# A scalar on 128 partitions: a broadcast load at the head of the load queue instead of a matmul

## The chip, the core and the metric

The kernel runs on one core of one Trainium2 chip. The metric is the device time of one execution in microseconds (us); the time of a kernel is the median of several executions.

## What is computed

`x` and `fx` have the shape (512, 32, 640) in bf16, `alpha` has one bf16 element. The result has the shape and type of `x`:

```python
def reference(x, fx, alpha):
    return x + alpha * fx
```

Each of the three large arrays is 10,485,760 elements, 20.97 MB. Two are read and one is written, 62.9 MB in all.

## The kernel before

Each array is seen as 128 rows of 81,920 elements, one row for each SBUF partition, and cut along the row into five chunks of `CHUNK = 16384` elements. A chunk is a tile of 128 x 16384 bf16, 32 KB in each partition and 4096 KB in all. The tiles of `x` come from a pool `xs` with four buffers, those of `fx` from a pool `fs` with two. The result overwrites the tile of `x`, and this tile is stored.

For chunk k, `compute(k)` is one VectorE instruction (L69, `scalar_tensor_tensor`), which reads `f_t`, multiplies by the scalar `a_f`, adds `x_t` and writes `x_t`. The scalar has to stand in each of the 128 partitions as an f32 value. The last chunk is computed and stored in two halves.

All ten loads (L59 for `x`, L63 for `fx`) and all six stores (L80) are issued by SyncE, in an order that is written out by hand, as no scheduler moves anything:

```python
    load_x(0)
    load_f(0)
    load_x(1)
    load_f(1)
    load_x(2)
    compute(0)
    load_f(2)
    store(0)
    load_x(3)
    compute(1)
```

It goes on in the same way to `store(4, 0, 2)` and `store(4, 1, 2)`. SyncE waits ahead of an issue where that issue needs it: a load of `fx` for the compute that frees its buffer, the fifth load of `x` for the first store, and a store for its compute.

Ahead of all this, `alpha_to_lanes` brings the scalar to the partitions. ScalarE issues a DMA that loads the one element into one partition (L20); VectorE fills a row of 128 ones (L22); TensorE multiplies the two, which leaves alpha in 128 partitions of PSUM (L24); VectorE copies it to `a_f` in SBUF (L26). The lines L120 and L131 are those of the program's start and end.

Of the kernel before, what the change touches and what calls it, by code (L numbers as in the profile page):

```python
# [1 line left out]

# [4 lines left out]

ACT = mybir.ActivationFunctionType
ALU = mybir.AluOpType
F32 = mybir.dt.float32  # L10
BF16 = mybir.dt.bfloat16

CHUNK = 16384


def alpha_to_lanes(nc, consts, psum, alpha, eng):

    P = nc.NUM_PARTITIONS
    a_1 = consts.tile([1, 1], alpha.dtype, name="a_1")
    eng.dma_start(out=a_1[:], in_=alpha[None, :])  # L20
    ones = consts.tile([1, P], alpha.dtype, name="ones")
    nc.vector.memset(ones[:], 1.0)  # L22
    a_ps = psum.tile([P, 1], F32, name="a_ps")
    nc.tensor.matmul(a_ps[:], ones[:], a_1[:], start=True, stop=True)  # L24
    a_f = consts.tile([P, 1], F32, name="a_f")
    nc.vector.tensor_copy(out=a_f[:], in_=a_ps[:])  # L26
    return a_f


@with_exitstack  # L30
def kernel(
    ctx: ExitStack,
    tc: tile.TileContext,
    x: bass.AP,
    fx: bass.AP,
    alpha: bass.AP,
    out: bass.AP,
):
    nc = tc.nc
    P = nc.NUM_PARTITIONS  # L40
    xv = x.flatten_outer_dims().rearrange("(p n) d -> p (n d)", p=P)
    fxv = fx.flatten_outer_dims().rearrange("(p n) d -> p (n d)", p=P)
    ov = out.flatten_outer_dims().rearrange("(p n) d -> p (n d)", p=P)
    F = xv.shape[1]
    K = F // CHUNK
    assert K * CHUNK == F and K == 5

    consts = ctx.enter_context(tc.tile_pool(name="consts", bufs=1))
    psum = ctx.enter_context(tc.tile_pool(name="psum", bufs=1, space=bass.MemoryType.PSUM))
    xs = ctx.enter_context(tc.tile_pool(name="xs", bufs=4))  # L50
    fs = ctx.enter_context(tc.tile_pool(name="fs", bufs=2))
    ctx.enter_context(tc.manual_schedule())

    a_f = alpha_to_lanes(nc, consts, psum, alpha, nc.scalar)
    xt, ft = {}, {}

    def load_x(k):
        xt[k] = xs.tile([P, CHUNK], x.dtype, tag="x", name="x_t")
        nc.sync.dma_start(out=xt[k][:], in_=xv[:, bass.ts(k, CHUNK)])  # L59

    def load_f(k):
        ft[k] = fs.tile([P, CHUNK], fx.dtype, tag="f", name="f_t")
        nc.sync.dma_start(out=ft[k][:], in_=fxv[:, bass.ts(k, CHUNK)])  # L63

    def compute(k, parts=1):
        n = CHUNK // parts
        for j in range(parts):
            s = bass.ts(j, n)
            nc.vector.scalar_tensor_tensor(  # L69
                out=xt[k][:, s],  # L70
                in0=ft[k][:, s],
                scalar=a_f[:],
                in1=xt[k][:, s],
                op0=ALU.mult,
                op1=ALU.add,
            )

    def store(k, j=0, parts=1):
        n = CHUNK // parts
        nc.sync.dma_start(  # L80
            out=ov[:, k * CHUNK + j * n : k * CHUNK + (j + 1) * n],
            in_=xt[k][:, bass.ts(j, n)],
# [12 lines that stand above are left out]
    load_f(3)  # L95
    store(1)
    load_x(4)
    compute(2)
    load_f(4)
    store(2)  # L100
    compute(3)
    store(3)
    compute(4, 2)
    store(4, 0, 2)
    store(4, 1, 2)


# [1 line left out]
_INS = ['x', 'fx', 'alpha']  # L109
_OUTS = [((512, 32, 640), 'bfloat16')]  # L110


# [23 lines left out]
```

## Time and profile before

| | |
|---|---|
| median of 4 runs | 152.68 us (152.46 to 153.14) |
| the profiled execution's own time | 152.58 us |
| its span, from the first to the last instruction | 150.8 us |
| busy: VectorE, TensorE | 86.9 us, 0.2 us |
| moved by DMA | 62.92 MB, mean 417 GB/s over the span |
| 128x16384 instruction of L69 | 17.28 us each, four of them |
| 128x8192 instruction of L69 | 8.75 us each, two of them |

The profile is one execution; its own time and its span differ by what lies before the first and after the last instruction. In the lines of the profile, SPq and ACTq are the instruction queues of SyncE and ScalarE, where DMAs are issued, and DVE is VectorE, PE and PEld are TensorE's matmuls and weight loads. The duration beside a DMA issue is that of the issue alone; the data moves afterwards, on 16 DMA engines. q1 is the DMA queue that SyncE feeds and q10 the one that ScalarE feeds.

### The profile page before, as it was taken

How to read it: one execution, taken by the hardware profiler on the slowest of the kernel's cores; microseconds unless marked ns; L12 is line 12 of the kernel's file. 1: busy time of each engine (PE TensorE's matmuls, PEld its weight loads, DVE VectorE, ACT ScalarE, POOL GpSimd, SP SyncE). 2: the span in 40 equal slices, each digit the busy share in tenths (PEclk: the TensorE clock that was granted, in tenths of full speed). 3: DMA queues.
4: the chain of work that ended last, by engine and by line, in shares of the span. 5: the costliest groups of instructions: out<-in, count | busy, mean ns of one | idle time of the engine just before them, and what ended most of it. 6: DMA issues, size and time to landing. Idle time of an engine off the chain costs nothing.

```text
span 150.8 us, 85 instructions
## 1 busy us (share of the span) xinstructions
PE 0.2 (0%) x1; PEld 0.1 (0%) x1; DVE 86.9 (58%) x8; POOL 0.2 (0%) x4
## 2 busy tenths in 40 slices
PE   0000000000000000000000000000000000000000
PEld 0000000000000000000000000000000000000000
DVE  0000009999679998399991006999900089997000
POOL 0000000000000000000000000000000000000000
DMA  6999999999999999899999999999999999998994
GB/s 217 435 426 443 426 417 417 452 443 435 435 452 417 426 417 391 365 435 443 435 435 417 417 417 435 452 452 426 435 426 435 417 426 426 452 443 387 435 435 196
DMA packets 2306, 62.92 MB, mean 417 GB/s; under 512 B 258, under 2 KB 258, under 8 KB 258
## 3 DMA queue, kind: packets, MB, share of 16 engines
q1 hardware_dynamic: 2304, 62.92, 97.9%
q10 hardware_dynamic: 2, 0.00, 0.0%
HBM read 41.94 MB, written 20.97 MB: 417 GB/s over the span
## 4 chain that ended last, share of the span: by engine, by line
DMA 56%; DVE 29%; DVEq 6%; issue 0%; SPq 0%
DMA f_t<-in_fx_dram 56%; DVE x_t L69 29%; DVEq L131 6%; SPq L59 0%; DVEq L69 0%
## 5 line engine op out<-in xcount | busy, mean ns | idle before, releaser
L69 DVE SCALAR_TENSOR_TENSOR x_t<-f_t,a_f,x_t 128x16384 bf16<-128x16384 bf16 (+1 forms) x6 | 86.6, 14440 | 49.7 <-DMA f_t<-in_fx_dram 49.7
L26 DVE COPY a_f<-a_ps 128x1 f32<-128x1 f32 x1 | 0.2, 159 | 1.1 <-PE a_ps L24 1.1
L22 DVE MEMSET ones<- 1x128 bf16 x1 | 0.2, 165 | 0.8 <-PEq L120 0.8
L24 PE MATMUL a_ps<-a,ones 1*128 1x1 bf16 x1 | 0.2, 159 | 1.9 <-DMA a<-in_alpha_dram 1.9
L120 POOL MEMSET const-bfloat16-1.0<- 128x1 bf16 x1 | 0.1, 101 | 0.0
L120 POOL MEMSET const-uint8-127<- 128x1 uint8 x1 | 0.1, 101 | 0.0
L24 PEld LDWEIGHTS <-ones 1*128 1x128 bf16 x1 | 0.1, 99 | 1.0 <-DVE ones L22 1.0
L120 POOL MEMSET const-float32-0.0<- 128x1 f32 x1 | 0.1, 98 | 0.2 <-issue 0.2
L120 POOL MEMSET const-float32-1.0<- 128x1 f32 x1 | 0.1, 98 | 0.0
## 6 DMA issues: line engine op xcount, KB each, us to landing
x_t<-in_x_dram SPq DMA_DIRECT2D x5, 4096.0 KB, 34.8
f_t<-in_fx_dram SPq DMA_DIRECT2D x5, 4096.0 KB, 32.2
out_dram<-x_t SPq DMA_DIRECT2D x4, 4096.0 KB, 36.6
out_dram<-x_t SPq DMA_DIRECT2D x2, 2048.0 KB, 15.2
a<-in_alpha_dram ACTq DMA_DIRECT2D x1, 0.0 KB
```

What stands on the lines that cost most here:

```text
L22: nc.vector.memset(ones[:], 1.0)
L24: nc.tensor.matmul(a_ps[:], ones[:], a_1[:], start=True, stop=True)
L26: nc.vector.tensor_copy(out=a_f[:], in_=a_ps[:])
L69: nc.vector.scalar_tensor_tensor(out=xt[k][:, s], in0=ft[k][:, s], scalar=a_f[:], in1=xt[k][:, s], op0=ALU.mult, op1=ALU.add,)
L120: nc = _bacc.Bacc("TRN2", target_bir_lowering=False, num_devices=1)
L131: with _tile.TileContext(nc) as tc:
```

## The change

`alpha_to_lanes` no longer uses TensorE. One DMA reads the single element of alpha 128 times and writes it to one bf16 column `a_b` of 128 partitions, and VectorE copies this column to `a_f` in f32. The DMA is issued by SyncE instead of ScalarE, and as `alpha_to_lanes` is called first, its issue comes ahead of `load_x(0)` on the same queue. The row of ones, the matmul and the PSUM pool are gone. The order of all loads, computes and stores is as it was. The lines after the function stand five lines higher: L54, L58, L64 and L75 for what was L59, L63, L69 and L80.

```diff
-def alpha_to_lanes(nc, consts, psum, alpha, eng):
+def alpha_to_lanes(nc, consts, alpha, eng):
 
     P = nc.NUM_PARTITIONS
-    a_1 = consts.tile([1, 1], alpha.dtype, name="a_1")
-    eng.dma_start(out=a_1[:], in_=alpha[None, :])
-    ones = consts.tile([1, P], alpha.dtype, name="ones")
-    nc.vector.memset(ones[:], 1.0)
-    a_ps = psum.tile([P, 1], F32, name="a_ps")
-    nc.tensor.matmul(a_ps[:], ones[:], a_1[:], start=True, stop=True)
+    a_b = consts.tile([P, 1], alpha.dtype, name="a_b")
+    eng.dma_start(out=a_b[:], in_=alpha.to_broadcast((P, 1)))
     a_f = consts.tile([P, 1], F32, name="a_f")
-    nc.vector.tensor_copy(out=a_f[:], in_=a_ps[:])
+    nc.vector.tensor_copy(out=a_f[:], in_=a_b[:])
     return a_f
...
     consts = ctx.enter_context(tc.tile_pool(name="consts", bufs=1))
-    psum = ctx.enter_context(tc.tile_pool(name="psum", bufs=1, space=bass.MemoryType.PSUM))
...
-    a_f = alpha_to_lanes(nc, consts, psum, alpha, nc.scalar)
+    a_f = alpha_to_lanes(nc, consts, alpha, nc.sync)
```

## The prediction, made before the changed kernel was run

> **What bounds the kernel now.** I read the page's header, the slices and the queues first, to see which resource is never idle.
>
> ```profile
> span 150.8 us, 85 instructions
> PE 0.2 (0%) x1; PEld 0.1 (0%) x1; DVE 86.9 (58%) x8; POOL 0.2 (0%) x4
> DMA  6999999999999999899999999999999999998994
> GB/s 217 435 426 443 426 417 417 452 443 435 435 452 417 426 417 391 365 435 443 435 435 417 417 417 435 452 452 426 435 426 435 417 426 426 452 443 387 435 435 196
> ...
> q1 hardware_dynamic: 2304, 62.92, 97.9%
> q10 hardware_dynamic: 2, 0.00, 0.0%
> ```
>
> A slice is 150.8/40 = 3.77 us. The 16 DMA engines are busy from the first slice to the last; VectorE is busy 58%. All data is on one queue, q1, that of SyncE: 62.92 MB. From slice 2 to slice 39 the rate is about 425 GB/s, so the bytes alone need 62.92/0.425 = 148 us of the 150.8. The two weak slices at the ends are the start-up and the completion, and a delay at the start can only matter if nothing later has slack that takes it up.
>
> The second view is the groups with what they wait for, and the chain of work that ended last.
>
> ```profile
> L69 DVE SCALAR_TENSOR_TENSOR x_t<-f_t,a_f,x_t 128x16384 bf16<-128x16384 bf16 (+1 forms) x6 | 86.6, 14440 | 49.7 <-DMA f_t<-in_fx_dram 49.7
> ...
> L26 DVE COPY a_f<-a_ps 128x1 f32<-128x1 f32 x1 | 0.2, 159 | 1.1 <-PE a_ps L24 1.1
> DMA f_t<-in_fx_dram 56%; DVE x_t L69 29%; DVEq L131 6%; SPq L59 0%; DVEq L69 0%
> ```
>
> VectorE waited 49.7 us for `f_t` and never for `a_f` after the start. The chain names VectorE for 29%, yet in that time the queue has work. I count what SyncE has issued against what has moved. Five loads (21.0 MB) are issued in the first 3.2 us and last until 21.0/0.425 = 49 us; the next issues come at 40.2 us, when the first compute ends. By 79.9 us, when the last `f_t` load goes out, 11 transfers (46.1 MB) are issued and about 33 MB have moved. At 129.8 us, when the first half of the last store is released, 14 transfers (58.7 MB) are issued and 128 x 0.427 = 55 MB have moved. So the queue does not run dry until the last half store, issued at 138.5 us, and **the stream of transfers is one serial resource from its first packet to its last**.
>
> The third view is the timeline of the start.
>
> ```profile
> 0.73 0.38 SPq L59 DMA_DIRECT2D x_t<-in_x_dram  x1
> 0.73 0.49 ACTq L20 DMA_DIRECT2D a<-in_alpha_dram  x1
> 0.81 0.17 DVE L22 MEMSET ones<- 1x128 bf16 x1 [0.81 <-PEq L120]
> 1.03 0.10 PEld L24 LDWEIGHTS <-ones 1*128 1x128 bf16 x1 [1.03 <-DVE ones L22]
> 1.16 0.42 SPq L63 DMA_DIRECT2D f_t<-in_fx_dram  x1
> 1.64 0.42 SPq L59 DMA_DIRECT2D x_t<-in_x_dram  x1
> 1.92 0.16 PE L24 MATMUL a_ps<-a,ones 1*128 1x1 bf16 x1 [1.92 <-DMA a<-in_alpha_dram]
> ...
> 2.12 0.16 DVE L26 COPY a_f<-a_ps 128x1 f32<-128x1 f32 x1 [1.14 <-PE a_ps L24]
> ...
> 22.92 17.28 DVE L69 SCALAR_TENSOR_TENSOR x_t<-f_t,a_f,x_t 128x16384 bf16<-128x16384 bf16 x1 [20.64 <-DMA f_t<-in_fx_dram]
> ```
>
> The columns are start, duration, engine, line and operation. SyncE issues the first load of `x` at 0.73 us, beside ScalarE's issue of alpha. `a_f` is ready at 2.28 us; its first reader starts at 22.92 us. When do the loads begin to move? Stretches of a tenth of a microsecond (last columns: clock, DMA share, GB/s) put the first data packets of 32 KB at 1.7 to 2.1 us, that is about 1.0 us after the issue starts:
>
> ```profile
> 1.60:1.70 0.10, 0.00 (x0) 0.00 (x0) 0.00 (x0) 0.00 (x0) 1.00 0.00 0
> 1.70:1.80 0.10, 0.00 (x0) 0.00 (x0) 0.00 (x0) 0.00 (x0) 1.00 6.85 1966
> ```
>
> (A packet is booked whole where it starts, hence a share above 1.)
>
> **What the Trainium skill says.** All from its page "DMA: Bandwidth & Descriptors".
> - Section "Issuing engines are not separate DMA queues": DMAs of several issuing engines run on the same 16 DMA engines, and a second issuer "will only save the time on the sequencer it takes to initiate the DMA". The trace agrees: ScalarE's 0.49 us lie beside SyncE's first 0.38 us. This saving is what the change gives up.
> - Section "Why a DMA increments its semaphore by 16 and not by 1": a copy of 128 partitions is split over 16 engines, a [1, 1] scalar runs on one. The counts agree: q10 has 2 packets (data and semaphore), and q1 has 2304 = 16 transfers x (128 rows + 16 semaphore packets).
> - Section "Measured", under "Bandwidth": 4 KB to 128 partitions takes 0.68 us on the DMA engines (for DMAs issued by GpSimd). No small 128-partition transfer is in the trace of before; I use this as a price.
>
> **The change part by part.**
> 1. Removed: the memset of `ones` (0.17 us), the weight load (0.10), the matmul (0.16), the wait for it (1.1), the PSUM tile. All of it is over by 2.3 us and hidden under the first two loads, for which VectorE waits until 22.92. Worth 0. If that cover were gone it would be some 1.4 us on VectorE.
> 2. The copy to `a_f` (0.16 us) now waits for the broadcast. That lands at about 0.73 + 1.19 (issue to landing of the scalar, 1.92 - 0.73) + 0.68 = 2.6 us, with 20 us to spare. VectorE holds nothing else before it. Cost 0.
> 3. One DMA issue moves from ScalarE's queue to the head of SyncE's and so ahead of all 16 issues there; `x` 0 to `x` 2 all start later by it. POOL's four memsets are not passed. The pitch of issues on SyncE at the start is 1.16 - 0.73 = 0.43 and 1.64 - 1.16 = 0.48 us, ScalarE's issue took 0.49. I take **0.45 us**. Bounds: the shortest and longest issue on SyncE in the trace, 0.33 and 0.73 us.
> 4. The scalar's single packet becomes 128 packets of 2 bytes and 16 for the semaphore, nine on each of the 16 engines, ahead of the first data packet. They can start where the first load's packets do now, at 1.7 us, and the price of 0.68 us takes them to 2.38. The first load's packets are ready at 1.70 + 0.45 = 2.15. What sticks out is 2.38 - 2.15 = **0.23 us**. Bounds: 0, if nine packets pass within the 0.45 us (50 ns each), and about 1.1 us if the engines start the load only after the broadcast has landed (case C below). A gain is not in this term: packets are only added to q1.
> 5. Buffers and waits: the order of SyncE's issues and the waits for computes and for freed buffers stay the same. The removed PSUM tile frees nothing that is waited for.
>
> Sum: 0 + 0 + 0.45 + 0.23 = **+0.68 us**. As the queue always holds a backlog, nothing later absorbs it: the landings of `f_t`, the computes and the stores shift together. The profiled execution took 152.58 us (1.78 us around its span); it would take 153.26. It lies 0.10 under the median of the four runs, 152.68, so for the median I say **153.36 us**. That is +0.45%; a measurement of this kernel can tell about 0.3%, or 0.46 us, from no change, so the effect is not far beyond what can be seen.
>
> **The rivals.**
> - B, hidden at the start. After the first packets at 1.7 to 2.5 us no further one starts until 3.25 us, though a 32 KB packet needs only 32768 B/(425/16 GB/s) = 1.23 us. The first ended at 1.7 + 1.23 = 2.93 at the earliest, most next ones start in 3.50 to 3.75, so the start-up has some 0.4 us of slack of its own. If that pause is a first-access cost that the tiny packets pay instead, 0.68 - 0.4 leaves +0.28: 152.96 us, no visible change. Against it: the pause may well follow the first large packets wherever they start.
> - C, a stall of the rings. If the 2-byte writes are slow, or each engine's semaphore write, which has to follow its data, holds up what lies behind it, the load's packets start only when the broadcast has landed, about 2.6 us, and their own latency after that is only partly hidden. Landing instead of 1.7 costs 0.9, and up to 0.6 us of the 1.0 between issue and first packet again: +1.5, 154.18 us. Against it: in the steady stream semaphore packets follow each transfer and the rate stays near 425.
> - D, faster. The rate dips where the 16 engines fall out of step: slices 16 and 17 (391 and 365 GB/s) and slice 37 (387) lose (39 + 65 + 43)/430 x 3.77 = 1.3 us. Slice 37, 135.7 to 139.5 us, lies where the last store is released with little backlog left. If alpha's packet on a second queue, on one engine only, is what sets this engine back at the start, an even load on all 16 would shrink the dips. It decides once it gains more than the 0.46 us of the bound and what step 3 and 4 still cost, 0.28 with the start as in B, together 0.74 us. With two thirds of the 1.3 gone the balance is 0.28 - 0.9 = about -0.62: 152.06 us. For it: only that a single slow engine delays every landing. Against it: one packet of 2 bytes is small beside 120 packets of 32 KB per engine, and nothing ties the dips to it.
> - That the change does not do what it says: the broadcast may be issued on SyncE at no more than the scalar's cost and run on few engines. The order of issues in the changed program has it first, so this ends in A or B.
>
> **How the numbers follow.** A (+0.68) 0.50, B (+0.28) 0.25, C (+1.5) 0.13, D (-0.62) 0.12. Hence slower by over 0.3%: A and C, 0.63; within 0.3%: B, 0.25; faster: D, 0.12. A alone spans 152.68 + 0.33 = 153.01 to 152.68 + 0.73 + 0.23 = 153.64. The range takes in B down to the undisturbed scatter of the runs (lowest 152.46) and C with its bound, and leaves D out: 152.5 to 154.3.
>
> **What would show it.** Right: the first line of the timeline is the issue of `a_b` on SyncE at 0.73, the first load's issue is at about 1.18, the first large packets at about 2.4, the first compute at about 23.6, and every later compute about 0.7 later with no new wait; the small packets on q1 grow by 144 (258 - 2 + 144 = 400) and q10 is gone. Wrong at step 3: an issue of the broadcast over 0.73 us or under 0.33. Wrong at step 4: large packets that start at 2.15 or before, or after 3 us. Wrong about the serial stream: a first compute that is later and a last store that is not. Wrong altogether: a last compute earlier than 121.07 us.

## The result and the profile after

Over 42 executions of the changed kernel and 61 of the kernel before, the medians are 153.10 and 152.69 us: +0.41 us. The ratio is 1.0029, 95% interval 1.0019 to 1.0039, that is 0.29 to 0.60 us slower in this round (a second round, below, shows less). The profiled executions took 152.85 and 152.58 us, both a little below their medians.

The page of the changed kernel, its totals, slices, queues, chain and groups:

```profile
span 151.1 us, 81 instructions
DVE 86.7 (57%) x7; POOL 0.2 (0%) x4
DMA  5999999999999999999999999999999999999995
GB/s 139 382 425 443 416 416 417 425 460 443 451 425 434 417 416 416 417 416 416 434 469 451 451 416 417 416 417 416 451 460 443 451 416 416 417 416 430 425 443 230
...
q1 hardware_dynamic: 2448, 62.92, 97.5%
...
DMA f_t<-in_fx_dram 56%; DVE x_t L64 29%; DVEq L126 6%; SPq L54 0%; SPq L20 0%; DVEq L64 0%
L64 DVE SCALAR_TENSOR_TENSOR x_t<-f_t,a_f,x_t 128x16384 bf16<-128x16384 bf16 (+1 forms) x6 | 86.5, 14439 | 48.2 <-DMA f_t<-in_fx_dram 48.2
```

The bound is the same: the DMA engines are busy in every slice and VectorE waits for `f_t`. TensorE is gone from the list, q10 from the queues, and q1 has 2448 - 2304 = 144 more packets, as counted. Three slices tell of the change. The first moves 139 GB/s instead of 217: the stream starts later. Slices 16 and 17, which were 391 and 365, are 416 and 417: **the dip is gone at this scale**, and the sum of the prediction had nothing for that. Slice 37 rises too, from 387 to 430, but from the start of the fifth compute to the end of the span both kernels take 29.7 us, so it is worth nothing here.

The timeline of the start and of the large computes:

```profile
0.72 0.54 SPq L20 DMA_DIRECT2D a_b<-in_alpha_dram  x1
1.32 0.56 SPq L54 DMA_DIRECT2D x_t<-in_x_dram  x1
...
3.94 0.15 DVE L22 CAST a_f<-a_b 128x1 f32<-128x1 bf16 x1 [3.94 <-DMA a_b<-in_alpha_dram]
24.06 17.28 DVE L64 SCALAR_TENSOR_TENSOR x_t<-f_t,a_f,x_t 128x16384 bf16<-128x16384 bf16 x1 [19.97 <-DMA f_t<-in_fx_dram]
...
43.46 17.29 DVE L64 SCALAR_TENSOR_TENSOR x_t<-f_t,a_f,x_t 128x16384 bf16<-128x16384 bf16 x1 [2.11 <-DMA f_t<-in_fx_dram]
...
63.08 17.29 DVE L64 SCALAR_TENSOR_TENSOR x_t<-f_t,a_f,x_t 128x16384 bf16<-128x16384 bf16 x1 [2.34 <-DMA f_t<-in_fx_dram]
```

The kernel before has the second and third compute here:

```profile
42.31 17.28 DVE L69 SCALAR_TENSOR_TENSOR x_t<-f_t,a_f,x_t 128x16384 bf16<-128x16384 bf16 x1 [2.10 <-DMA f_t<-in_fx_dram]
62.60 17.29 DVE L69 SCALAR_TENSOR_TENSOR x_t<-f_t,a_f,x_t 128x16384 bf16<-128x16384 bf16 x1 [3.01 <-DMA f_t<-in_fx_dram]
```

And the stretches of a tenth of a microsecond in which the data of the changed kernel starts (before: 1.70):

```profile
2.40:2.50 0.10, 0.00 (x0) 0.00 (x0) 1.00 0.07 0
2.50:2.60 0.10, 0.00 (x0) 0.00 (x0) 1.00 5.81 1311
```

The first load is issued 0.59 us later (1.32 against 0.73), its packets start 0.8 us later, and the first compute starts 1.14 us later (24.06 against 22.92). The records of single packets in the two traces show where the rest comes from: the 2-byte packets run from 2.0 to 3.5 us, and the first sixteen packets of 32 KB start at 2.5 to 3.7 us, where it was 1.7 to 2.4. The first of them is 0.8 us late, the sixteenth 1.3. The second compute is still 1.15 late. The third, at 63.08, is only 0.48 late, and the last two 0.32 and 0.36 (92.19 against 91.87, 121.43 against 121.07). So the start cost more than forecast, and 0.67 us of it came back between the second and the third compute. The kernel before shows why in the same stretch (clock, DMA share and GB/s are the last three columns):

```profile
57.00:58.00 1.00, 0.00 (x0) 0.00 (x0) 1.00 (x1) 0.00 (x0) 1.00 0.79 328
58.00:59.00 1.00, 0.00 (x0) 0.00 (x0) 1.00 (x1) 0.00 (x0) 1.00 1.61 492
59.00:60.00 1.00, 0.00 (x0) 0.00 (x0) 0.59 (x1) 0.00 (x0) 1.00 1.00 295
60.00:61.00 1.00, 0.00 (x0) 0.00 (x0) 0.00 (x0) 0.00 (x0) 1.00 0.74 229
```

In these four microseconds it moves 336 GB/s on average instead of 425, a loss of 4 x (1 - 336/425) = 0.84 us, while the engines count as fully busy: packets run long, they are not missing. In the trace's records some thirty packets of 32 KB, about two for each of the 16 engines, take 1.3 to 2.1 us there instead of 1.21. I call this the pause. The third compute waits for an `f_t` whose last packets lie in it. The changed kernel, a microsecond later, loses 4 x (1 - 393/425) = 0.30 us, so in this profile a rest of the pause is left:

```profile
58.00:59.00 1.00, 1.00 (x1) 0.00 (x0) 1.00 1.22 524
59.00:60.00 1.00, 1.00 (x1) 0.00 (x0) 1.00 1.37 524
60.00:61.00 1.00, 0.74 (x1) 0.00 (x0) 1.00 0.91 328
61.00:62.00 1.00, 0.00 (x0) 0.00 (x0) 1.00 0.53 197
```

### The profile page after: what moved, and what is told of

Read it like the earlier page. It is cut to its first block, busy times and chain, and to the rows that moved or that the text cites. A ratio compares the mean times of both kernels' runs of the same rounds, so it can differ in the third digit from the quotient of the medians.

```text
span 151.1 us, 81 instructions
## 1 busy us (share of the span) xinstructions
DVE 86.7 (57%) x7; POOL 0.2 (0%) x4
## 2 busy tenths in 40 slices
DMA packets 2448, 62.92 MB, mean 416 GB/s; under 512 B 400, under 2 KB 400, under 8 KB 400
## 3 DMA queue, kind: packets, MB, share of 16 engines
q1 hardware_dynamic: 2448, 62.92, 97.5%
## 4 chain that ended last, share of the span: by engine, by line
DMA 56%; DVE 29%; DVEq 6%; SPq 1%; issue 0%
DMA f_t<-in_fx_dram 56%; DVE x_t L64 29%; DVEq L126 6%; SPq L54 0%; SPq L20 0%; DVEq L64 0%
## 5 line engine op out<-in xcount | busy, mean ns | idle before, releaser
L64 DVE SCALAR_TENSOR_TENSOR x_t<-f_t,a_f,x_t 128x16384 bf16<-128x16384 bf16 (+1 forms) x6 | 86.5, 14439 | 48.2 <-DMA f_t<-in_fx_dram 48.2
```

Of the source, the lines that this page charges most:

```text
L64: nc.vector.scalar_tensor_tensor(out=xt[k][:, s], in0=ft[k][:, s], scalar=a_f[:], in1=xt[k][:, s], op0=ALU.mult, op1=ALU.add,)
```

## The experiments

They asked three things: how the 1.14 us at the start divide between the place in the queue and the broadcast's packets; whether a late start is handed on whole; and what the pause is and what shortens it. Two numbers of each profile carry the answers: the start of the first compute, and the distance from the second compute to the third, which is 19.4 us where no packet runs long and longer by the pause.

### Both kernels again

> The kernel before, unchanged, profiled a second time. Theory 1 (the pause near 58 to 61 us, in which the packets of the third fx tile ran long, is a disturbance of one execution and has nothing to do with the start): ratio 1.000 within 0.002; the first compute again near 22.9 us; the pause comes out with another size or elsewhere, so the third compute starts anywhere from 61.7 to 62.7 us. Theory 2 (the pause belongs to the order of the transfers, and a later start makes it shorter): ratio 1.000; the third compute again at 62.6 us within 0.1.

> The changed kernel, profiled a second time. Both theories: about 1.003 of the kernel before. Theory 1: the first compute again near 24.06 us (+1.14 over before), and the delay seen in the third compute differs from the first profile's +0.48 by some tenths, as the pause is drawn anew. Theory 2: the first compute at +1.14, the third again at +0.5 within 0.15, so that 0.6 to 0.7 us is given back at the same place.

The kernel before has a ratio to itself of 0.9993 (0.9978 to 1.0008). Its second profile:

```profile
22.70 17.28 DVE L69 SCALAR_TENSOR_TENSOR x_t<-f_t,a_f,x_t 128x16384 bf16<-128x16384 bf16 x1 [20.42 <-DMA f_t<-in_fx_dram]
42.09 17.29 DVE L69 SCALAR_TENSOR_TENSOR x_t<-f_t,a_f,x_t 128x16384 bf16<-128x16384 bf16 x1 [2.11 <-DMA f_t<-in_fx_dram]
62.50 17.28 DVE L69 SCALAR_TENSOR_TENSOR x_t<-f_t,a_f,x_t 128x16384 bf16<-128x16384 bf16 x1 [3.12 <-DMA f_t<-in_fx_dram]
```

The second profile of the changed kernel:

```profile
24.16 17.29 DVE L64 SCALAR_TENSOR_TENSOR x_t<-f_t,a_f,x_t 128x16384 bf16<-128x16384 bf16 x1 [19.87 <-DMA f_t<-in_fx_dram]
43.55 17.28 DVE L64 SCALAR_TENSOR_TENSOR x_t<-f_t,a_f,x_t 128x16384 bf16<-128x16384 bf16 x1 [2.11 <-DMA f_t<-in_fx_dram]
63.00 17.29 DVE L64 SCALAR_TENSOR_TENSOR x_t<-f_t,a_f,x_t 128x16384 bf16<-128x16384 bf16 x1 [2.16 <-DMA f_t<-in_fx_dram]
```

The pair repeats. The first compute is 1.46 us late (1.14 in the first pair), the third 0.50 (0.48); the distance from second to third shrinks from 20.41 to 19.45 us (20.29 to 19.62). The give-back, 0.67 and 0.96 us, belongs to the change: theory 1, a disturbance of one execution, falls. By the last compute the second pair is down to 0.16 us (121.53 against 121.37), the first to 0.36; these last tenths differ between profiles of one kernel (121.07 and 121.37 before), and no experiment asked for them.

The time of this second round, with 14 executions, gives medians of 153.03 and 152.81 us, 0.22 apart, and a ratio of 0.9998 (0.9981 to 1.0015). This interval doesn't meet the one above (1.0019 to 1.0039), so the two rounds differ by more than either interval allows for; the kernel before, unchanged, has medians from 152.69 to 152.97 us over the five rounds. I keep +0.41, from the 42 executions, as the result. That the changed kernel is slower is likely, and its size is known only to some 0.3 us, the spread of these medians.

### The place alone, and the broadcast alone

```diff
# in the kernel before
-    a_f = alpha_to_lanes(nc, consts, psum, alpha, nc.scalar)
+    a_f = alpha_to_lanes(nc, consts, psum, alpha, nc.sync)
```

> The place alone: the scalar load and the matmul stay, but the scalar's DMA is issued by SyncE ahead of the first load. Its issue took 0.49 us on ScalarE, the pitch of issues is 0.43 to 0.48. Theory P (the cost of the change is the place in the queue): the first load is issued 0.5 to 0.6 us later, the first compute starts at +0.5 to +0.6, time 1.002 to 1.004. Theory B (the cost is the 128 tiny packets and their semaphore packets): the first compute below +0.2, time 1.000 to 1.001.

```diff
# in the changed kernel
-    a_f = alpha_to_lanes(nc, consts, alpha, nc.sync)
+    a_f = alpha_to_lanes(nc, consts, alpha, nc.scalar)
```

> The broadcast alone: 128 packets of 2 bytes instead of one, but issued by ScalarE on its own queue, beside the first load. Theory P: the first load is issued at 0.73 us as before, the first compute within 0.2 us of before, time 1.000 to 1.001. Theory B: the tiny packets interleave with the first data packets or share the generation of descriptors, the first compute at +0.5 to +0.7 us, time 1.002 to 1.004. If the two effects add up to the changed kernel's +1.14, each of the two parts shows about half.

The scalar's load at the head of SyncE's queue:

```profile
0.73 0.34 SPq L20 DMA_DIRECT2D a<-in_alpha_dram  x1
...
1.12 0.36 SPq L59 DMA_DIRECT2D x_t<-in_x_dram  x1
...
23.19 17.29 DVE L69 SCALAR_TENSOR_TENSOR x_t<-f_t,a_f,x_t 128x16384 bf16<-128x16384 bf16 x1 [20.87 <-DMA f_t<-in_fx_dram]
```

The place costs 0.39 us of issue and 0.27 to 0.49 us at the first compute, less than the 0.5 to 0.6 of theory P and more than the 0.2 of theory B; the pause stays in full (20.30 us from second to third). The medians are 153.05 and 152.81 us, the ratio 1.0016 (0.9990 to 1.0041): the size fits, the time alone doesn't prove it.

The broadcast on ScalarE's queue:

```profile
15.82 0.15 DVE L22 CAST a_f<-a_b 128x1 f32<-128x1 bf16 x1 [15.82 <-DMA a_b<-in_alpha_dram]
24.41 17.29 DVE L64 SCALAR_TENSOR_TENSOR x_t<-f_t,a_f,x_t 128x16384 bf16<-128x16384 bf16 x1 [8.44 <-DMA f_t<-in_fx_dram]
43.81 17.28 DVE L64 SCALAR_TENSOR_TENSOR x_t<-f_t,a_f,x_t 128x16384 bf16<-128x16384 bf16 x1 [2.12 <-DMA f_t<-in_fx_dram]
63.24 17.29 DVE L64 SCALAR_TENSOR_TENSOR x_t<-f_t,a_f,x_t 128x16384 bf16<-128x16384 bf16 x1 [2.15 <-DMA f_t<-in_fx_dram]
```

The first load is issued at 0.73 us, as before, and still the first compute is 1.49 to 1.71 us late, against the two profiles of the kernel before; theory B had 0.5 to 0.7. The tiny packets take turns with the 32 KB packets: in the trace's records the 128 of them start over 4.7 to 14.3 us, the first seven rounds of 16 some 1.2 to 1.5 us apart, about as long as one 32 KB packet takes. Alpha lands at 15.8 us instead of 1.9. The pause is gone: 19.43 us from second to third. The ratio of the time is 1.0030 (1.0015 to 1.0046). So it is the broadcast, not the place, that shortens the pause. The two parts, 0.3 to 0.5 and 1.5 to 1.7, come to more than the changed kernel's 1.14 to 1.46. A likely reason, not tested, is that at the head of the queue the later issue of the load is hidden in part: it would let the 32 KB packets start at 2.3 us (1.0 after the issue), and they start at 2.5 to 3.7, behind the tiny ones.

### A pure delay, more broadcasts, a later broadcast, a later store

```diff
# in the kernel before
     def load_x(k):
         xt[k] = xs.tile([P, CHUNK], x.dtype, tag="x", name="x_t")
+        if k == 0:
+            nc.vector.memset(xt[0][:, 0:2048], 0.0)
```

> The kernel before with a pure delay: VectorE fills the first 2048 columns of the first x tile with zeros, and the load that overwrites them waits for that, some 0.8 to 1.4 us. No small packet is added. Theory S (the stream is serial and hands a late start on; the pause at 58 to 61 us is cut by the broadcast's packets, not by lateness): the first compute later by the delay d that the timeline shows, the third and the last compute later by d within 0.2 us, the pause as long as before (third compute 20.4 us after the second), time 152.7 + d. Theory L (lateness itself shortens the pause): the third compute starts only d - 0.6 or so later, time within 0.3% of before for d near 1.

```diff
# in the changed kernel
-    a_b = consts.tile([P, 1], alpha.dtype, name="a_b")
-    eng.dma_start(out=a_b[:], in_=alpha.to_broadcast((P, 1)))
+    for i in range(4):
+        a_b = consts.tile([P, 1], alpha.dtype, name=f"a_b{i}")
+        eng.dma_start(out=a_b[:], in_=alpha.to_broadcast((P, 1)))
```

> The changed kernel with four broadcasts of alpha at the head of SyncE's queue instead of one. One costs 0.6 us of issue and 1.14 to 1.2 us at the first compute. Theory S: each further one costs its issue or its packets, 0.6 to 0.8 us, so the first compute at 25.9 to 26.6 us; the pause is already short and can give back 0.4 us at the most, so the last compute at 123.0 to 123.9 and the time 154.6 to 155.6 us. Theory L: part of the further delay is given back as well, time 153.1 to 154.0 us.

```diff
# in the changed kernel
-    a_f = alpha_to_lanes(nc, consts, alpha, nc.sync)
...
     load_x(0)
+    a_f = alpha_to_lanes(nc, consts, alpha, nc.sync)
     load_f(0)
```

> The changed kernel with the broadcast issued second, after the first load of x; its packets lie between the first x tile and the first fx tile on each engine. The first load is then issued at 0.73 us as before. Theory S: the small packets still cost their own time on the engines, the first compute at +0.4 to +0.7 over before instead of +1.14, and if the broadcast's packets anywhere ahead shorten the pause near 58 us, the third compute comes 19.6 us after the second and the last compute at -0.3 to 0: time 0.997 to 1.000 of before. Theory L: the pause goes with the start, 20.4 us between the second and third compute, time 1.002 to 1.004.

```diff
# in the kernel before
     load_f(2)
+    load_x(3)
     store(0)
-    load_x(3)
```

> The kernel before with two issues of SyncE exchanged: the fourth load of x is issued ahead of the first store. The pause near 58 to 61 us lies in the last two packets of each engine ahead of the first store. Theory W (it belongs to the first store, the first writes of the run): it moves by one tile to about 68 to 71 us, and the third compute comes at about 61.6 us instead of 62.6. Theory T (it belongs to this tile of fx or to this time): it stays at 58 to 61 us and the third compute at 62.5 us. Time in both within 0.3% of before.

The delay came out larger than meant, since VectorE reached the memset only behind the copy to `a_f`: the first load was issued at 3.37 us, d = 2.64:

```profile
3.37 0.38 SPq L61 DMA_DIRECT2D x_t<-in_x_dram  x1
...
25.50 17.28 DVE L71 SCALAR_TENSOR_TENSOR x_t<-f_t,a_f,x_t 128x16384 bf16<-128x16384 bf16 x1 [22.16 <-DMA f_t<-in_fx_dram]
44.89 17.29 DVE L71 SCALAR_TENSOR_TENSOR x_t<-f_t,a_f,x_t 128x16384 bf16<-128x16384 bf16 x1 [2.11 <-DMA f_t<-in_fx_dram]
65.38 17.28 DVE L71 SCALAR_TENSOR_TENSOR x_t<-f_t,a_f,x_t 128x16384 bf16<-128x16384 bf16 x1 [3.20 <-DMA f_t<-in_fx_dram]
```

The first compute is 2.58 us later and the third 2.78, and the medians are 155.60 and 152.97 us: +2.63 (ratio 1.0155, 1.0109 to 1.0202, from 6 executions). A late start is handed on whole, and lateness leaves the pause as it is (20.49 us). Theory L falls.

With four broadcasts:

```profile
0.72 2.47 SPq L21 DMA_DIRECT2D a_b<-in_alpha_dram  x4
3.23 0.59 SPq L55 DMA_DIRECT2D x_t<-in_x_dram  x1
...
28.12 17.29 DVE L65 SCALAR_TENSOR_TENSOR x_t<-f_t,a_f,x_t 128x16384 bf16<-128x16384 bf16 x1 [19.41 <-DMA f_t<-in_fx_dram]
47.54 17.28 DVE L65 SCALAR_TENSOR_TENSOR x_t<-f_t,a_f,x_t 128x16384 bf16<-128x16384 bf16 x1 [2.13 <-DMA f_t<-in_fx_dram]
66.98 17.28 DVE L65 SCALAR_TENSOR_TENSOR x_t<-f_t,a_f,x_t 128x16384 bf16<-128x16384 bf16 x1 [2.15 <-DMA f_t<-in_fx_dram]
```

The first compute starts 4.06 us later than with one broadcast, 1.35 us for each further one; an issue is 0.62 to 0.64 of that (0.72 to 3.23 us for four). The median is 157.12 us, 4.0 above the changed kernel's. Once the pause is gone (19.44 us), nothing more comes back, as theory S has it; but each one is dearer than the 0.6 to 0.8 that I gave it, and the time is over the 154.6 to 155.6 us of that theory.

With the broadcast second, `x` is issued at 0.72 us:

```profile
24.55 17.28 DVE L63 SCALAR_TENSOR_TENSOR x_t<-f_t,a_f,x_t 128x16384 bf16<-128x16384 bf16 x1 [9.69 <-DMA f_t<-in_fx_dram]
43.95 17.29 DVE L63 SCALAR_TENSOR_TENSOR x_t<-f_t,a_f,x_t 128x16384 bf16<-128x16384 bf16 x1 [2.12 <-DMA f_t<-in_fx_dram]
63.38 17.28 DVE L63 SCALAR_TENSOR_TENSOR x_t<-f_t,a_f,x_t 128x16384 bf16<-128x16384 bf16 x1 [2.14 <-DMA f_t<-in_fx_dram]
```

The first compute starts **1.63 to 1.85 us late without any delay of the first issue**, more than at the head and far over the 0.4 to 0.7 expected. The pause is gone (19.43 us). The medians are 153.82 and 152.97 us, the ratio 1.0053 (1.0033 to 1.0074), where theory S had 0.997 to 1.000. The last compute starts at 121.97 us, later than in the changed kernel (121.43 and 121.53), but the intervals of the two ratios overlap, so that it is slower than the changed kernel is likely and not shown.

With the first store one place later, the slices of the page show where the pause went: slices 16 and 17 are 425 and 460, and slice 19 is 338.

```profile
GB/s 225 434 434 434 416 416 425 442 460 434 434 442 416 416 416 425 460 442 338 416 416 425 460 408 460 416 442 416 434 425 425 451 460 416 425 434 412 416 421 165
```

```profile
42.16 17.28 DVE L69 SCALAR_TENSOR_TENSOR x_t<-f_t,a_f,x_t 128x16384 bf16<-128x16384 bf16 x1 [2.11 <-DMA f_t<-in_fx_dram]
61.59 17.29 DVE L69 SCALAR_TENSOR_TENSOR x_t<-f_t,a_f,x_t 128x16384 bf16<-128x16384 bf16 x1 [2.14 <-DMA f_t<-in_fx_dram]
91.88 17.28 DVE L69 SCALAR_TENSOR_TENSOR x_t<-f_t,a_f,x_t 128x16384 bf16<-128x16384 bf16 x1 [13.01 <-DMA f_t<-in_fx_dram]
```

The third compute comes 19.43 us after the second, and the fourth 30.29 us after the third, where it was 29.27. The pause moved with the store, in the one profile taken: **it lies ahead of the first store of the run**, theory W. The median is 152.58 us, ratio 0.9979 (0.9959 to 0.9999). As the last compute starts at 121.37 us, no earlier than in the kernel before (121.07 and 121.37), I don't count this as a gain.

### What in the broadcast shortens the pause

The kernel before, with one more transfer issued by ScalarE behind the scalar's load, one packet for each of the 16 engines:

```diff
+    w_src = consts.tile([16, 512], x.dtype, name="w_src")
+    nc.gpsimd.memset(w_src[:], 0.0)
+    w_dst = consts.tile([16, 512], x.dtype, name="w_dst")
+    nc.scalar.dma_start(out=w_dst[:], in_=w_src[:])
```

> The kernel before, and behind the scalar's load ScalarE issues a copy from SBUF to SBUF of 16 rows of 1 KB (filled by GpSimd, read by nobody): one packet for each DMA engine, near 2 us. Theory R (the pause ahead of the first store is the engines' first read of SBUF[...]): the pause is gone, the third compute 19.4 us after the second instead of 20.4, the first compute within 0.3 us of before, the last near 120.3 us, time 0.993 to 0.997. Theory H (the pause is the first write to HBM): the pause stays at 1.0 us, time 1.000 to 1.003. Theory Q (small packets[...] take the pause away by something else than a read of SBUF): as H here.

```diff
+    w_dst = consts.tile([16, 1], x.dtype, name="w_dst")
+    nc.scalar.dma_start(out=w_dst[:], in_=xv[0:16, 0:1])
```

> The kernel before, and behind the scalar's load ScalarE issues a load of 16 rows of 2 bytes of x into 16 partitions (read by nobody): one small packet for each DMA engine, no broadcast. Theories R and Q: the pause ahead of the first store is gone, the third compute 19.4 us after the second, time 0.993 to 0.998. If only the many packets or the repeated source address of the broadcast do it: the pause stays (20.4 us), time 1.000 to 1.003.

```diff
+    w_dst = consts.tile([16, 512], x.dtype, name="w_dst")
+    nc.scalar.dma_start(out=w_dst[:], in_=xv[0:16, 0:512])
```

> Control: the same as the load of 16 rows of 2 bytes, with rows of 1 KB. Theories R and Q: no read of SBUF and no small packet, so the pause stays, the third compute 20.4 us after the second, time 0.999 to 1.002. If any extra transfer on all 16 engines ahead takes the pause away: 19.4 us, time 0.993 to 0.998.

And the scalar's load itself widened to 16 partitions:

```diff
-    a_1 = consts.tile([1, 1], alpha.dtype, name="a_1")
-    eng.dma_start(out=a_1[:], in_=alpha[None, :])
+    a_16 = consts.tile([16, 1], alpha.dtype, name="a_16")
+    eng.dma_start(out=a_16[:], in_=alpha.to_broadcast((16, 1)))
...
-    nc.tensor.matmul(a_ps[:], ones[:], a_1[:], start=True, stop=True)
+    nc.tensor.matmul(a_ps[:], ones[:], a_16[0:1, :], start=True, stop=True)
```

> The kernel before with the scalar's load widened to 16 partitions on ScalarE's queue: one 2-byte packet of alpha for each DMA engine, the matmul reads row 0; nothing else changes. Theory A (each engine's first access to the memory where alpha lies, next to the result's, pays ahead what the first store otherwise pays): the pause ahead of the first store is gone, the third compute 19.4 to 19.6 us after the second, the first compute within 0.3 us of before, time 0.992 to 0.996, faster than both kernels. Theory N (it takes the broadcast's number of packets or of partitions, whatever their source): the pause stays at 1.0 us, third compute 20.4 us after the second, time 0.999 to 1.002.

| profile | first compute | second to third | ratio of the time |
|---|---|---|---|
| before (two profiles) | 22.92, 22.70 | 20.29, 20.41 | |
| changed kernel (two) | 24.06, 24.16 | 19.62, 19.45 | 1.0029 (1.0019 to 1.0039), 0.9998 (0.9981 to 1.0015) |
| copy from SBUF, 16 x 1 KB | 22.96 | 20.09 | 1.0003 (0.9987 to 1.0019) |
| load, 16 x 2 bytes | 22.79 | 20.64 | 0.9995 (0.9969 to 1.0021) |
| load, 16 x 1 KB | 22.92 | 20.03 | 0.9998 (0.9979 to 1.0017) |
| alpha on 16 partitions | 22.88 | 20.62 | 0.9996 (0.9975 to 1.0018) |

The queue q10 of the copy's run and of the run with alpha on 16 partitions, and the timeline of the latter:

```profile
q10 hardware_dynamic: 34, 0.02, 0.0%
```

```profile
q10 hardware_dynamic: 32, 0.00, 0.0%
```

```profile
8.21 0.16 PE L24 MATMUL a_ps<-a,ones 1*128 1x1 bf16 x1 [8.21 <-DMA a<-in_alpha_dram]
...
42.28 17.29 DVE L69 SCALAR_TENSOR_TENSOR x_t<-f_t,a_f,x_t 128x16384 bf16<-128x16384 bf16 x1 [2.12 <-DMA f_t<-in_fx_dram]
62.90 17.28 DVE L69 SCALAR_TENSOR_TENSOR x_t<-f_t,a_f,x_t 128x16384 bf16<-128x16384 bf16 x1 [3.33 <-DMA f_t<-in_fx_dram]
```

None of the four removes the pause, and none changes the time. q10 has 2 packets for the scalar before; the copy adds 32, and alpha on 16 partitions has 32 in all, which is 16 of data and 16 for the semaphore, one for each engine as the prediction read such counts. So the copy reads SBUF on all engines, and alpha's packets come from all of them: theory R (first read of SBUF) and theory A (first access beside alpha) fall. A small packet on each engine is not enough either, so theory Q, as I put it, falls too. The two transfers of 1 KB leave some 0.3 us less of the pause, from one profile each. The last line of the table also shows what a packet on all engines does to a small load beside a large stream: with alpha on 16 partitions the matmul starts at 8.21 us instead of 1.92.

What is shown: with alpha broadcast to 128 partitions, in five profiles of four kernels, the distance is 19.43 to 19.62 us; without it and with the first store in its place, in eight profiles of seven kernels, 20.03 to 20.64. What is left for a cause is the number of packets, the number of partitions written, or the repeated source at that number. Which of these, and by what mechanism in the engines, **stays open**: no run loads 128 different elements, and none broadcasts to a number of partitions between 16 and 128. Nor is it shown whether the broadcast takes the pause away or only pays for it earlier, within its own cost at the start. Against the second stands that each further broadcast in the run with four cost 1.35 us, as much as the first one (1.14 to 1.46), and not some 1.0 us less.

## Why the prediction was right, point by point

The forecast was +0.68 us for the median, and +0.41 (0.29 to 0.60) was measured: the direction and the order of size are right, and the value lies inside the range, as does the second round. But it is right for a sum in which two errors nearly cancel: the start cost 1.14 us instead of 0.68, and 0.67 came back of which the sum knew nothing. That the two are of one size is luck.

- Steps 1, 2 and 5 held. The matmul path was worth nothing: with alpha on 16 partitions its copy to `a_f` ran only at 8.41 us, and the first compute started at 22.88 all the same. The changed kernel's copy had 20 us to spare: it ran at 3.94 us, later than the 2.6 estimated. No new wait appeared.
- Step 3, the issue: 0.45 forecast, 0.60 measured (0.72 to 1.32 us), inside its bounds. In the run with the scalar it was 0.39.
- Step 4, the packets: 0.23 forecast; 1.14 - 0.60 = 0.54 measured, and 1.46 - 0.59 = 0.87 in the second pair. The price from the Trainium skill ("DMA: Bandwidth & Descriptors", section "Measured": 0.68 us for 4 KB to 128 partitions) was for DMAs issued by GpSimd and too low here: the prediction had the small packets from 1.70 to 2.38 us, and they ran from 2.0 to 3.5; between two large tiles the broadcast cost 1.63 us. This is the mis-sized term. The sign that I had named for it, large packets that start after 3 us, missed it, as it looked at the first of them alone.
- "As the queue always holds a backlog, nothing later absorbs it" is the step that failed. The backlog was there, and the delay run shows that a late start is passed on whole. What I had not seen is that the stream's own pace could change: the broadcast takes 0.67 to 0.96 us out of the pause ahead of the first store. With these measured terms the sum is 1.14 - 0.67 = 0.47, and 1.46 - 0.96 = 0.50, at the third compute; what takes it down to 0.36 and 0.16 at the fifth is not explained.
- Rival B gave +0.28 by slack in the start-up. The time is between A and B, but B's mechanism was not there: the first compute was later, not earlier, than A had it. B read the gap after the first packets as slack; the trace's records show long packets there, 1.7 to 2.2 us for each of the first sixteen instead of 1.21. One broadcast leaves them long (1.2 to 2.4). Behind four they take 1.21 to 1.32, in one profile; whether the tiny packets do that or the longer wait since the issue is not shown.
- Rival C, the engines holding the load back until the broadcast has landed: not as stated. The first large packets start at 2.5 us and alpha lands at 3.94. But the sixteenth starts only at 3.7, which is 1.3 us later than before and close to the 1.5 that C had for the whole load. That fits step 4 coming out larger.
- Rival D named the right place, the dip in slices 16 and 17, and a gain there did come. Its cause, the single packet of alpha on one engine, falls: with alpha on all 16 engines the dip stays.

Of the signs I had named, "every later compute about 0.7 later" was the one that gave the error away: the five computes were 1.14, 1.15, 0.48, 0.32 and 0.36 us later, in the second pair 1.46, 1.46, 0.50, 0.32 and 0.16.

## What to carry to other kernels

When one resource is serial from start to end, ask of an added transfer not only what it delays but whether the pace of the stream changes, and compare the delay at several stages of the profile rather than at the end alone. Of the three places tried for the broadcast of one element the head of the queue was the cheapest: there it cost 1.1 to 1.5 us at the first compute, 1.5 to 1.7 on another queue beside the stream and 1.6 to 1.9 between two tiles. A scalar that needs one partition only, spread by a matmul that nothing waits for, put one packet of data and one for the semaphore on the engines, for which the trace's records have 0.01 us each; no run leaves it out, so what it costs the stream is not measured.

## What the hardware did that I had not expected

- Ahead of the first store the stream of loads slows for some three microseconds, while the engines count as busy; packets of 32 KB take up to 2.1 us instead of 1.21. It costs 0.9 to 1.0 us in the kernel before and moves with the store by one tile (slice 19 at 338 GB/s instead of slices 16 and 17).
- A broadcast of one element to 128 partitions, in any of three places ahead of it, takes most or all of that away, while one small packet on each engine doesn't (19.4 to 19.6 us against 20.0 to 20.6).
- 128 packets of 2 bytes, 256 bytes in all, cost 1.63 us or more between two tiles, in which time the stream would move 0.7 MB at 425 GB/s.
